# Moving the bursts of small matmuls, two transposes and the last output pieces in a fused attention and MLP kernel

## The chip, the core and the metric

The kernel runs on one core of a Trainium2 chip. The metric is device time in microseconds (us) from the program's start to its end. Before the change the median of three runs is 246.94 us (246.36 to 247.11). One further execution was taken with the hardware profiler; all durations below come from it.

The engines are named as in the profile: PE multiplies matrices (TensorE), with PEld loading its weights; DVE (VectorE) and ACT (ScalarE) read and write on-chip memory element by element; POOL (GpSimd) and SP (SyncE) here mostly issue DMA transfers. Each engine runs its instructions in program order and waits on semaphores of the others.

## The reference

There are 8 batches of 8 heads, 576 positions and head size 64, and 32 packed queries `p` per head. `sm_attn` is softmax attention with scale 1/8.

```python
p_packed = sm_attn(p, k, v)             # 32 x 64 per head
out = sm_attn(q, p_packed, p_packed)    # 576 x 64 per head
x = out.transpose(0, 2, 1, 3).reshape(4608, 512)
h = x @ w_in                            # 512 -> 2048
g = h * cos(h)
result = g @ w_out                      # 2048 -> 512, float32
```

All inputs are float32; the kernel casts them to bfloat16 while they are loaded.

## The kernel before, in words

**Per batch `b`.** A load brings k, q and v of the batch in (three DMAs issued by POOL, `load`, L92). k and q are needed transposed: batches 3 and up do it by a DMA transpose issued by SP (`xbar`, L96), k of batch 2 by PE (`pe_T`, L103) in three groups of eight 96x96 transposes, each group copied out of PSUM by DVE or ACT. `s1(b)` (L142) multiplies packed queries by k and ACT takes the exponential into `a1`. `a1` is transposed into `a1T`, from batch 3 on by a DMA transpose (`a1_xbar`, L158). `pp(b)` (L173) is the packed product, `a1T` by v: 48 small matmuls and two small copies into `pp_sb`; `pp_T` (L188) transposes it into `ppT`. `s2(b)` (L221) gives the second scores, `sums2` and `normalise` the normalised weights `a2n`. `ppw(b, n)` (L195) multiplies `ppT` by quarter n of `w_in`: 8 matmuls into one PSUM pair and one cast of 128x1024 into the columns 512n to 512n+511 of `PPW[b]`, so the second attention and `w_in` are folded into one matrix.

**A slot.** `slot(s, ...)` (L486) runs 16 steps, fc = 0 to 15, for batch s. Step fc computes the hidden block h(fc) on PE (`h_mm`, L250: four matmuls of 288 columns with columns 128·fc to 128·fc+127 of `PPW[s]`), its cosine on ACT (L261) and the product g(fc) on DVE (L264). So the `PPW` quarter n=2 is first needed at step 8. Between the hidden blocks PE does *out products*, the 128x512 matmuls of `g @ w_out` (L345) of the batch before, handed out one by one by `fill(n)`; 16 of them make one chunk of 128 output rows, which is copied out of PSUM into `osb` (by ACT inside a slot, by DVE between slots) and stored by two DMAs that SP issues. The slot spreads the out products over the steps by weights: `heavy={5: (5, 3)}` gives step 5 five extra shares, with 3 of its out products placed behind what hangs on that step.

**The burst.** `hooks` hang other work on a step. `tiled(s)` (L507) is the burst: `ppw(s, 2)` and `ppw(s, 3)`, 16 matmuls of a 64x32 form, then `pp(s+1)`, 48 of a 96x32 form, whose result goes into the spare columns of the hidden block's own PSUM pair (`spare`). In slot 2 it hangs on step 6, in slots 3 to 6 on step 5. ACT casts quarter 2, DVE does the two `pp_sb` copies and casts quarter 3.

**Between slots** come the `s2`, `sums2`, `normalise`, `ppw(b, 0)` and `ppw(b, 1)` of the next batch, the `s1` and `a1_xbar` of the one after, with out products between them. This stretch for batch 2 (L533 to L567) is written out by hand; L571 to L602 do it for the others.

**PSUM.** One pool of three pairs of banks (`psA`) is taken in rotation by everything but the out products: an allocation waits until the reader of the third one before it is done, so h(k) waits for g(k-3) if nothing came between. The out products have two banks of their own (`ot`).

**Queues.** SP issues stores and DMA transposes strictly in program order, and a wait of one holds all behind it. POOL issues the loads; before each set of three a one-element copy from `kT` of a later batch into `gate` (L528, L564, L588) holds POOL until that transpose has landed.

**The tail.** `tail_chunk` (L325) makes the last 128 rows in two pieces of 256 columns: 16 matmuls, a copy (ACT, then DVE) and two stores, one each from SP and ACT.

Of the kernel before, what the change touches and what calls it, by code (L numbers as in the profile page):

```python
# [8 lines left out]
FP32 = mybir.dt.float32  # L9
BF16 = mybir.dt.bfloat16  # L10
# [5 lines left out]
def kernel(  # L16
# [17 lines left out]
    TP = S // C  # L34
# [15 lines left out]
    O = ctx.enter_context(tc.tile_pool(name="psO", bufs=2, space=PSUM))  # L50
# [12 lines left out]
    V, ACT, G = nc.vector, nc.scalar, nc.gpsimd  # L63
# [5 lines left out]
    gate = const.tile([1, 1], BF16, name="gate")  # L69
# [10 lines left out]
    bf, xT, a1T, sums1, r1, rs1 = {}, {}, {}, {}, {}, {}  # L80
    a2u, lns, a2n, PPW = {}, {}, {}, {}

    def copy(eng, out, in_):
        if eng is ACT:
            ACT.copy(out=out, in_=in_)  # L85
        else:
            eng.tensor_copy(out=out, in_=in_)  # L87

    def psa(dt=FP32):
        return psum["A"].tile([128, 2, 512 if dt == FP32 else 1024], dt, name="psA", tag="A")  # L90

    def load(n, b):  # L92
        bf[n, b] = bf_pool.tile([TP, H, C * D], BF16, name=n + "bf", tag=n + "bf", bufs=1 if n == "q" else 2)
        G.dma_start(out=bf[n, b], in_=srcs[n][b].rearrange("h (p c) d -> p h (c d)", c=C))

    def xbar(n, b):  # L96
        t = xT[n, b] = att_pool.tile([128, H * 3, TP], BF16, name=n + "T", tag=n + "T", bufs=2 if n == "k" else 1)
        nc.sync.dma_start_transpose(out=t, in_=bf[n, b].rearrange("p h x -> p (h x)"))
# [4 lines left out]
    def pe_T(n, b, engs=(V, V, V), groups=(0, 1, 2), own=None):  # L103
        if 0 in groups:
            xT[n, b] = att_pool.tile([128, H * 3, TP], BF16, name=n + "T", tag=n + "T", bufs=2 if n == "k" else 1)
        t = xT[n, b]
        flat = bf[n, b].rearrange("p h x -> p (h x)")
        for i in groups:
            ps = own(BF16) if own else psa(BF16)[:, 0, :]
            for j in range(8):  # L110
                o = 8 * i + j
                nc.tensor.transpose(ps[:, j * TP:(j + 1) * TP], flat[:, o * 128:(o + 1) * 128],  # L112
                                    ident[0:TP, 0:TP])
            copy(engs[i], t[:, 8 * i:8 * i + 8].rearrange("p a x -> p (a x)"),
                 ps[:, 0:8 * TP])

    def bank(dt=FP32):
        return O.tile([128, 512 if dt == FP32 else 1024], dt, name="ot", tag="ot")
# [1 line left out]
    def pack_p(b0, b1, flat=None):  # L120
        ng = 2 * (b1 - b0)
        if flat is None:
            flat = psa(BF16).rearrange("p a x -> p (a x)")
        for g in range(ng):
            nc.tensor.transpose(flat[:, g * 128:(g + 1) * 128],
                                p_bf[:, 2 * b0 + g].rearrange("p t d -> p (t d)"), ident)
        V.tensor_copy(out=P2[:, b0:b1].rearrange("p b h n -> p (b h n)"), in_=flat[:, 0:ng * 128])
# [60 lines left out]
    def pp_T(b, eng=V, own=None):  # L188
        ps = own(BF16) if own else psa(BF16)[:, 0, :]
        t = pp_sb[b % 2].rearrange("p a d -> p (a d)")  # L190
        for i in range(2):
            nc.tensor.transpose(ps[:, i * 128:(i + 1) * 128], t[:, i * D:i * D + 128], ident)  # L192
        copy(eng, ppT[b % 2].rearrange("p i x n -> p (i x n)"), ps[:, 0:256])
# [98 lines left out]
    def h_rest(b):  # L292

        t = psa()
        for fc in range(NFC):
            for y in range(2):
                nc.tensor.matmul(t[:, fc // 8, (fc % 8) * 64:(fc % 8) * 64 + 64],
                                 PPW[b][:, y, fc * 128:(fc + 1) * 128], a2n[b][:, y, 512:576],
                                 start=(y == 0), stop=(y == 1))
        cs = cos_pool.tile([128, 2, 512], BF16, name="cosR", bufs=1)  # L300
        ACT.activation(out=cs, in_=t, func=AF.Sin, bias=PI_HALF)
        j0 = (b % 2) * 64
        V.tensor_tensor(out=joint[b // 2][:, :, j0:j0 + 64],
                        in0=t.rearrange("p a (f x) -> p (a f) x", x=64),
                        in1=cs.rearrange("p a (f x) -> p (a f) x", x=64), op=ALU.mult)
# [18 lines left out]

    def tail_chunk(b, c):  # L325
        osb = o_pool.tile([128, DM], FP32, name="osb")
        for i in range(2):
            cols = slice(i * 256, i * 256 + 256)
            ps = O.tile([128, 256], FP32, name="ot", tag="ot")
            for fc in range(NFC):  # L330
                nc.tensor.matmul(ps, joint[b // 2][:, fc, :], w_out_bf[:, fc, cols],  # L331
                                 start=(fc == 0), stop=(fc == NFC - 1))
            copy((ACT, V)[i], osb[:, cols], ps)
            for (a, z, rows), q in zip(pieces_of(b, c), (nc.sync, nc.scalar)):
                q.dma_start(out=rows[:, cols], in_=osb[a:z, cols])

# [25 lines left out]
    def fill(n):  # L362
        while n > 0 and filler:
            next(filler[0][0])
            filler[0][1] -= 1
            if filler[0][1] == 0:
                filler.pop(0)
            n -= 1
# [117 lines left out]
    def slot(s, hooks, keep=0, heavy={}, last=None):  # L486


        left = to_do() - keep
        weight = [1 + heavy.get(fc, (0, 0))[0] for fc in range(NFC)]  # L490
        for fc in range(NFC):
            rest = h_mm(s, fc)
            if fc == NFC - 1 and last:
                last()
            rest()
            quota = (left * sum(weight[:fc + 1])) // sum(weight) - (left + keep - to_do())
            behind = min(quota, heavy[fc][1]) if fc in heavy else quota
            fill(quota - behind)
            while hooks and hooks[0][0] == fc:
                hooks.pop(0)[1]()  # L500
            fill(behind)

    def pw2(b, n, eng=None):
        ppw(b, n, eng)
        ppw(b, n + 1, eng)

    def tiled(b):  # L507


        own, later = spare[0], []  # L510
        for n in (2, 3):
            later += ppw(b, n, (ACT, V)[n - 2], later=True)
        later[0]()
        pp(b + 1, V, own=lambda: own)
        later[1]()

    def tk(n, b, i):
        return lambda: pe_T(n, b, (ACT, V, ACT), (i,))

    def cross(n, b):  # L520
        return lambda: xbar(n, b)

    osb_eng[0] = ACT
    slot(1, [(2, lambda: pw2(1, 2, (ACT, V))), (4, lambda: h_rest(0)), (6, lambda: pack_p(2, 4)), (8, tk("k", 2, 0)), (9, tk("k", 2, 1)),
             (9, cross("q", 2)), (10, tk("k", 2, 2)), (12, cross("k", 3))], 4, {2: (1, 2), 4: (3, 5)})
    ACT.preload_act_table_set(EXP_SET)
    osb_eng[0] = V
    G.tensor_copy(out=gate, in_=xT["k", 3][0:1, 0, 0:1])  # L528
    load("v", 3)
    load("q", 3)  # L530
    load("k", 4)
# [6 lines left out]
    fill(3)  # L538
    a1_pe(2, (1,))
    recips(2)  # L540
    fill(5)
    pp(2)
    s1(3)
    a1_xbar(3)
    fill(3)
    pp_T(2)
    recips(3)
    fill(5)
    s2(2)
    ppw(2, 0, V)  # L550
    xbar("q", 3)
    xbar("k", 4)
    fill(3)
    sums2(2, 0)
    fill(3)
    sums2(2, 1)
    rest_ppw, = ppw(2, 1, (V, V), later=True)
    fill(2)
    normalise(2)
    ACT.preload_act_table_set(SIN_SET)  # L560
    rest_ppw()
    nc.sync.dma_start_transpose(out=P2[:, 4:B].rearrange("p b (t h) n -> p (b t) (h n)", t=2),
                                in_=p_bf[:, 8:2 * B].rearrange("p g t d -> p (g t d)"))
    G.tensor_copy(out=gate, in_=xT["k", 4][0:1, 0, 0:1])  # L564
    for n, b in (("v", 4), ("q", 4), ("k", 5)):
        load(n, b)
    fill(9)  # L567
    osb_eng[0] = ACT
    slot(2, [(6, lambda: tiled(2))], 10, {6: (5, 3)}, lambda: pp_T(3, V))

    for s in range(3, B):  # L571
        nxt = s + 1 < B
        ACT.preload_act_table_set(EXP_SET)
        osb_eng[0] = V
        set_filler(s - 1)
        fill(5)
        s2(s)
        ppw(s, 0, V)
        fill(8)
        if nxt:  # L580
            s1(s + 1)
            ppw(s, 1, V)
            a1_xbar(s + 1)
            xbar("q", s + 1)
            recips(s + 1)
            if s + 2 < B:
                xbar("k", s + 2)
                G.tensor_copy(out=gate, in_=xT["k", s + 2][0:1, 0, 0:1])  # L588
        else:
            for n in range(1, 4):  # L590
                ppw(s, n, V)
        fill(4 if nxt else 6)
        sums2(s, 0)
        fill(5)
        sums2(s, 1)
        normalise(s)
        ACT.preload_act_table_set(SIN_SET)
        fill(13)
        osb_eng[0] = ACT
        for n, b in (("v", s + 2), ("q", s + 2), ("k", s + 3)):  # L600
            if b < B:
                load(n, b)  # L602
        if nxt:
            slot(s, [(5, lambda: tiled(s))], 5 if s % 2 else 13, {5: (5, 3)}, lambda: pp_T(s + 1, V))
        else:
            slot(s, [], 5)
    set_filler(B - 1)
# [32 lines left out]
```

## Time and profile before

| what | us |
|---|---|
| median of three runs | 246.94 |
| the profiled execution, its whole time | 247.53 |
| its span, first to last instruction | 245.7 |
| PE busy | 232.0 |
| ACT busy | 166.6 |
| DVE busy | 162.4 |
| TensorE clock granted | 1.00 throughout |
| slot 2, its first hidden block | 74.95 |
| slot 3, its first hidden block | 101.71 |

Times in the text are counted from the start of the span. In a timeline a row gives start, length, engine, line, operation, tiles, shape and count; in brackets stands the idle time before it and what ended that. Matmuls are pipelined, and a matmul's length in a row includes its way through the array; what counts is the pitch from one start to the next: 216 ns for an out product, 122 ns for a matmul of 288 columns (0.49 us for a hidden block of four). Some matmul records are missing from a trace, so counts in rows may be one short of the program's. The chain of waits gives the work that ended last, in order of time, as start, length and name.

### The profile page before, as it was taken

Reading aid. Unit: us, or ns where it says so; the run is one execution under the profiler, and the core shown is the slowest. Engines: PE = TensorE matmul, PEld = TensorE weight load, DVE = VectorE, ACT = ScalarE, POOL = GpSimd, SP = SyncE. Lnnn points to the kernel's source line nnn. Section 1 sums busy time; section 2 is a strip of 40 time slices with the busy share of each in tenths; the row PEclk is TensorE's granted clock in tenths of the full one; section 3 lists DMA queues with packets and bytes.
Section 4 is the critical chain, followed back from the end, with each engine's and each line's share of the span. In section 5 each row is a group of like instructions: output and inputs, shape, how many; then the busy total and the mean of one; then the engine's idle time right before and its main releaser. Section 6 shows DMA issues by size and latency. Waiting matters only on the chain.

```text
span 245.7 us, 5424 instructions
## 1 busy us (share of the span) xinstructions
PE 232.0 (94%) x2204; PEld 128.4 (52%) x2239; DVE 162.4 (66%) x259; ACT 166.6 (68%) x267; POOL 38.1 (16%) x61
## 2 busy tenths in 40 slices
PE   7989889999999799999999999999999999999993
PEld 3463345566545464556455654656455645665452
DVE  3369987686459687578757875868656878784000
ACT  2359998767478587868786787858796766773110
POOL 8532330210130023004100510030100110011000
PEclk9999999999999999999999999999999999999999
DMA  6999999999789989999999799999292111311123
GB/s 87 204 210 207 204 208 227 200 240 149 167 121 185 215 182 197 215 204 174 163 191 237 134 214 207 189 161 179 56 194 51 37 45 43 85 39 49 54 74 85
DMA packets 63992, 37.37 MB, mean 152 GB/s; under 512 B 36592, under 2 KB 59376, under 8 KB 63968
## 3 DMA queue, kind: packets, MB, share of 16 engines
q0 software_dynamic: 23184, 18.81, 50.3%
q1 hardware_dynamic: 40624, 18.09, 35.9%
q8 instruction: 17, 0.28, 0.5%
q10 hardware_dynamic: 160, 0.13, 0.2%
q14 instruction: 7, 0.06, 0.1%
HBM read 37.22 MB, written 9.44 MB: 190 GB/s over the span
## 4 chain that ended last, share of the span: by engine, by line
PE 80%; DMA 13%; ACT 2%; issue 2%; DVE 1%; DVEq 0%
PE ot L345 45%; PE psA L257 21%; DMA qbf<-in_q_dram 7%; DMA a1T<-a 6%; PE ot L385 3%; PE psA L207 2%; PE psA L137 2%; PE psA L180 1%; PE ot L331 1%; PE psA L233 1%; PE psA L112 1%; ACT kT L85 1%; ACT a L146 1%; PE psA L192 0%; PE psA L170 0%
## 5 line engine op out<-in xcount | busy, mean ns | idle before, releaser
L345 PE MATMUL ot<-w_out_bf,gT 128*128 128x512 bf16 x483 | 127.3, 379 | 2.5 <-issue 2.1
L264 DVE TENSOR_TENSOR gT<-psA,cosT 128x576 bf16<-128x576 f32 x112 | 83.3, 757 | 19.5 <-ACT cosT L261 18.5
L261 ACT ACTIVATE cosT<-psA 128x576 bf16<-128x576 f32 x112 | 72.9, 652 | 24.8 <-PE psA L257 23.0
L257 PE MATMUL psA<-a2n,PPW 128*128 128x288 bf16 x448 | 73.3, 286 | 0.4 <-DVE gT L264 0.2
L345 PEld LDWEIGHTS <-gT 128*128 128x128 bf16 x512 | 48.1, 98 | 39.8 <-issue 4.4
L257 PEld LDWEIGHTS <-PPW 128*128 128x128 bf16 x448 | 43.7, 98 | 30.2 <-issue 0.6
L87 DVE CAST PPW<-psA 128x1024 bf16<-128x1024 f32 (+1 forms) x25 | 26.9, 1092 | 6.6 <-PE psA L207 6.4
L87 DVE COPY osb<-ot 128x512 f32<-128x512 f32 (+1 forms) x14 | 9.4, 670 | 20.6 <-PE ot L331 17.6
L85 ACT COPY osb<-ot 128x512 f32<-128x512 f32 (+1 forms) x23 | 13.2, 574 | 14.3 <-PE ot L345 13.2
L268 POOL COPY joint<-gT 128x512 bf16<-128x512 bf16 x14 | 8.6, 617 | 79.9 <-DVE gT L264 79.9
L243 DVE SCALAR_TENSOR_TENSOR a2n<-a2u,r,lns 128x576 bf16<-128x576 bf16 x16 | 12.4, 815 | 10.7 <-ACT lns L241 10.7
L146 ACT ACTIVATE a<-psA 128x576 bf16<-128x576 f32 x16 | 10.3, 646 | 7.8 <-PE psA L137 7.8
L235 ACT ACTIVATE lns<-psA 128x576 f32<-128x576 f32 x16 | 10.3, 650 | 7.2 <-PE psA L233 6.6
L345 PE MATMUL ot<-w_out_bf,joint 128*128 128x512 bf16 x47 | 12.0, 380 | 0.2
L225 ACT ACTIVATE a2u<-psA,rs 128x576 bf16<-128x576 f32 x16 | 11.0, 736 | 1.6 <-PE psA L137 1.4
L385 PE MATMUL ot<-wz 128*128 128x512 bf16 (+1 forms) x15 | 8.3, 660 | 2.0 <-DVE wz L399 1.7
L85 ACT CAST PPW<-psA 128x1024 bf16<-128x1024 f32 (+1 forms) x7 | 6.1, 891 | 5.8 <-PE psA L207 5.8
L241 ACT ACTIVATE lns<-lns 128x576 f32<-128x576 f32 x16 | 10.0, 674 | 0.0
L207 PE MATMUL psA<-w_in_bf,ppT 64*32 64x512 bf16 x224 | 9.8, 379 | 0.0
L289 DVE TENSOR_TENSOR gT<-psH,cosT 128x512 bf16<-128x512 f32 x15 | 9.3, 684 | 0.4 <-ACT cosT L288 0.4
L288 ACT ACTIVATE cosT<-psH 128x512 bf16<-128x512 f32 x15 | 8.4, 627 | 0.7 <-DVE gT L289 0.4
L588 POOL COPY gate<-kT 1x1 bf16<-1x1 bf16 x3 | 0.5, 181 | 50.8 <-DMA kT<-kbf 50.8
(92 smaller groups left out, 173.5 us busy)
## 6 DMA issues: line engine op xcount, KB each, us to landing
kbf<-in_k_dram POOLq DMA_DIRECT2D x8, 576.0 KB, 13.7
vbf<-in_v_dram POOLq DMA_DIRECT2D x8, 576.0 KB, 7.6
qbf<-in_q_dram POOLq DMA_DIRECT2D x8, 576.0 KB, 10.7
out_dram<-osb SPq DMA_DIRECT2D x24, 192.0 KB, 2.7
out_dram<-osb SPq DMA_DIRECT2D x22, 128.0 KB, 2.5
w_in_bf<-in_moe_w_in_dram POOLq DMA_DIRECT2D x4, 512.0 KB, 16.5
w_out_bf<-in_moe_w_out_dram POOLq DMA_DIRECT2D x4, 512.0 KB, 21.3
out_dram<-osb SPq DMA_DIRECT2D x26, 64.0 KB, 2.1
```

Of the source, the lines that this page charges most:

```text
L85: ACT.copy(out=out, in_=in_)
L87: eng.tensor_copy(out=out, in_=in_)
L146: ACT.activation(out=a1[b % 2][:, y, :, 0:TP].rearrange("p (e m) x -> p e m x", e=2), in_=ps[y][:, :, 0:HS].rearrange("p e (m x) -> p e m ...
L207: nc.tensor.matmul(ps[y][32 * x:32 * x + 32, :], ppT[b % 2][r, 0, x, :], w_in_bf[r, x, n * 512:(n + 1) * 512], start=True, stop=True)
L225: ACT.activation(out=a2u[b][:, y].rearrange("p (e x) -> p e x", e=2), in_=ps[y][:, :, 0:HS], func=AF.Exp, scale=rs1[b][:, y:y + 1])
L235: ACT.activation(out=lns[b][:, y].rearrange("p (e x) -> p e x", e=2), in_=ps[:, :, 0:HS], func=AF.Ln)
L243: V.scalar_tensor_tensor(out=a2n[b][:, y], in0=a2u[b][:, y], scalar=r1[b][:, y:y + 1], in1=lns[b][:, y], op0=ALU.mult, op1=ALU.mult)
L257: nc.tensor.matmul(ps[:, e, 0:HS], PPW[b][:, y, fc * 128:(fc + 1) * 128], a2n[b][:, y, e * HS:(e + 1) * HS], start=(y == 0), stop=(y == 1))
L261: ACT.activation(out=csv, in_=ps[:, :, 0:HS], func=AF.Sin, bias=PI_HALF)
L264: V.tensor_tensor(out=gT[b][:, fc, :].rearrange("p (e x) -> p e x", e=2), in0=ps[:, :, 0:HS], in1=csv, op=ALU.mult)
L345: nc.tensor.matmul(pss[c], w, w_out_bf[:, fc, :], start=(fc == 0), stop=(fc == NFC - 1))
L385: nc.tensor.matmul(wps, w[:, 0:128], w, start=True, stop=True)
```

## The change

- **Slots 3 to 6:** the burst `tiled(s)` hangs on step 7 in place of 5, with 4 out products behind it in place of 3.
- **Slot 2:** `ppw(2, 2)` and `ppw(2, 3)` stay on step 6, without `pp(3)`; quarter 2 is now cast by DVE and quarter 3 by ACT. `pp(3)` hangs alone on step 9, takes a PSUM pair of its own, and ACT does its two copies. The weights change to `{6: (3, 3), 9: (1, 1)}`.
- **k of batch 2 (slot 1):** groups 0 and 1 are both transposed at step 8, into the two halves of one PSUM pair, and then copied, one by ACT and one by DVE; group 2 stays on step 10. Step 9 has none any more.
- **Batch 2 between the slots:** seven out products in place of five before `pp(2)`, two for three and four for five behind it; `ppw(2, 1)` goes ahead of the second `sums2`, and DVE casts it whole at once, where it cast it in two halves after `normalise`. The total of out products is the same. On SP the two stores of one chunk now stand ahead of the transpose `a1T` of batch 3, where they stood behind it.
- **Batch 7:** one out product moves ahead of `ppw(7, 1)` to `ppw(7, 3)`.
- **Tail:** pieces of 256, 128 and 128 columns, copied by DVE, ACT, DVE; six stores for four.
- The `gate` copy gets a name, `behind`; its place and form are the same.

```diff
@@ pe_T
-            copy(engs[i], t[:, 8 * i:8 * i + 8].rearrange("p a x -> p (a x)"),
-                 ps[:, 0:8 * TP])
+            to = t[:, 8 * i:8 * i + 8].rearrange("p a x -> p (a x)"), ps[:, 0:8 * TP]
+            if engs[i] is None:
+                return to
+            copy(engs[i], *to)
@@ tail_chunk
-        for i in range(2):
-            cols = slice(i * 256, i * 256 + 256)
-            ps = O.tile([128, 256], FP32, name="ot", tag="ot")
+        for i, (a, z) in enumerate(((0, 256), (256, 384), (384, 512))):
+            cols = slice(a, z)
+            ps = O.tile([128, z - a], FP32, name="ot", tag="ot")
...
-            copy((ACT, V)[i], osb[:, cols], ps)
+            copy((V, ACT, V)[i], osb[:, cols], ps)
@@ slot 1
-    def tk(n, b, i):
-        return lambda: pe_T(n, b, (ACT, V, ACT), (i,))
+    def tk2():
+
+        t = psa(BF16)
+        later = []
+        for i in range(2):
+            later.append(pe_T("k", 2, (None,) * 3, (i,), own=lambda dt: t[:, i, :]))
+        for eng, (out, ps) in zip((ACT, V), later):
+            copy(eng, out, ps)
...
-    slot(1, [(2, lambda: pw2(1, 2, (ACT, V))), (4, lambda: h_rest(0)), (6, lambda: pack_p(2, 4)), (8, tk("k", 2, 0)), (9, tk("k", 2, 1)),
-             (9, cross("q", 2)), (10, tk("k", 2, 2)), (12, cross("k", 3))], 4, {2: (1, 2), 4: (3, 5)})
+    slot(1, [(2, lambda: pw2(1, 2, (ACT, V))), (4, lambda: h_rest(0)), (6, lambda: pack_p(2, 4)), (8, tk2),
+             (9, cross("q", 2)), (10, lambda: pe_T("k", 2, (V, V, ACT), (2,))), (12, cross("k", 3))], 4, {2: (1, 2), 4: (3, 5)})
@@ batch 2, between the slots
     recips(2)
-    fill(5)
+    fill(7)
     pp(2)
     s1(3)
     a1_xbar(3)
-    fill(3)
+    fill(2)
     pp_T(2)
     recips(3)
-    fill(5)
+    fill(4)
     s2(2)
...
     sums2(2, 0)
-    fill(3)
+    fill(1)
+    ppw(2, 1, V)
     sums2(2, 1)
-    rest_ppw, = ppw(2, 1, (V, V), later=True)
-    fill(2)
+    fill(4)
     normalise(2)
     ACT.preload_act_table_set(SIN_SET)
-    rest_ppw()
...
-    slot(2, [(6, lambda: tiled(2))], 10, {6: (5, 3)}, lambda: pp_T(3, V))
+    slot(2, [(6, lambda: pw2(2, 2)), (9, lambda: pp(3, ACT))], 10, {6: (3, 3), 9: (1, 1)}, lambda: pp_T(3, V))
@@ batches 3 to 7
-        fill(8)
+        fill(8 if nxt else 9)
...
-        fill(4 if nxt else 6)
+        fill(4 if nxt else 5)
...
-            slot(s, [(5, lambda: tiled(s))], 5 if s % 2 else 13, {5: (5, 3)}, lambda: pp_T(s + 1, V))
+            slot(s, [(7, lambda: tiled(s))], 5 if s % 2 else 13, {7: (5, 4)}, lambda: pp_T(s + 1, V))
```

More of the change, by code (lines that the diff above doesn't have):

```diff
@@ L94, in load, with behind @@
         G.dma_start(out=bf[n, b], in_=srcs[n][b].rearrange("h (p c) d -> p h (c d)", c=C))
+    def behind(t):
+        G.tensor_copy(out=gate, in_=t)
     def xbar(n, b):
@@ L523 @@
     osb_eng[0] = ACT
-    slot(1, [(2, lambda: pw2(1, 2, (ACT, V))), (4, lambda: h_rest(0)), (6, lambda: pack_p(2, 4)), (8, tk("k", 2, 0)), (9, tk("k", 2, 1)),
-             (9, cross("q", 2)), (10, tk("k", 2, 2)), (12, cross("k", 3))], 4, {2: (1, 2), 4: (3, 5)})
+    slot(1, [(2, lambda: pw2(1, 2, (ACT, V))), (4, lambda: h_rest(0)), (6, lambda: pack_p(2, 4)), (8, tk2),
+             (9, cross("q", 2)), (10, lambda: pe_T("k", 2, (V, V, ACT), (2,))), (12, cross("k", 3))], 4, {2: (1, 2), 4: (3, 5)})
     ACT.preload_act_table_set(EXP_SET)
     osb_eng[0] = V
-    G.tensor_copy(out=gate, in_=xT["k", 3][0:1, 0, 0:1])
+    behind(xT["k", 3][0:1, 0, 0:1])
     load("v", 3)
@@ L554 @@
     sums2(2, 0)
-    fill(3)
+    fill(1)
+    ppw(2, 1, V)
     sums2(2, 1)
-    rest_ppw, = ppw(2, 1, (V, V), later=True)
-    fill(2)
+    fill(4)
     normalise(2)
     ACT.preload_act_table_set(SIN_SET)
-    rest_ppw()
     nc.sync.dma_start_transpose(out=P2[:, 4:B].rearrange("p b (t h) n -> p (b t) (h n)", t=2),
                                 in_=p_bf[:, 8:2 * B].rearrange("p g t d -> p (g t d)"))
-    G.tensor_copy(out=gate, in_=xT["k", 4][0:1, 0, 0:1])
+    behind(xT["k", 4][0:1, 0, 0:1])
     for n, b in (("v", 4), ("q", 4), ("k", 5)):
@@ L587 @@
                 xbar("k", s + 2)
-                G.tensor_copy(out=gate, in_=xT["k", s + 2][0:1, 0, 0:1])
+                behind(xT["k", s + 2][0:1, 0, 0:1])
         else:
```

## The prediction

> **What bounds the kernel.** I read the page's busy times and its chain first, then PE's timeline stretch by stretch, then the rows of ACT, DVE and SP around each place that the change touches.
>
> ```profile
> PE 232.0 (94%) x2204; PEld 128.4 (52%) x2239; DVE 162.4 (66%) x259; ACT 166.6 (68%) x267; POOL 38.1 (16%) x61
> PE 80%; DMA 13%; ACT 2%; issue 2%; DVE 1%; DVEq 0%
> ```
>
> PE carries the chain. Between two hidden blocks PE's starts are as far apart as its pitches make them (216 ns an out product, 0.49 us a hidden block), so in such a stretch nothing can be won by moving work. Only the places count where a start comes late. Slot 1 has two, at the transposes of k:
>
> ```profile
> 53.40 0.65 PE L257 MATMUL psA<-a2n,PPW 128*128 128x288 bf16 x4
> 54.21 0.50 PE L112 MATMUL psA<-ident,kbf 96*128 96x96 bf16 x8 [0.16 <-ACT kT L85]
> ...
> 54.98 0.65 PE L257 MATMUL psA<-a2n,PPW 128*128 128x288 bf16 x4
> 55.58 0.50 PE L112 MATMUL psA<-ident,kbf 96*128 96x96 bf16 x8
> ```
>
> Four matmuls from 53.40 end by pitch at 53.89, and the transposes start at 54.21: 0.32 late. From 54.98 to 55.47, start at 55.58: 0.11 late. Slot 2 has two more:
>
> ```profile
> 76.89 0.59 PE L345 MATMUL ot<-w_out_bf,gT 128*128 128x512 bf16 x2
> 77.65 0.65 PE L257 MATMUL psA<-a2n,PPW 128*128 128x288 bf16 x4 [0.16 <-DVE gT L264]
> ...
> 81.86 0.63 PE L207 MATMUL psA<-w_in_bf,ppT 64*32 64x512 bf16 x16
> 83.68 0.56 PE L180 MATMUL psA<-vbf,a1T 96*32 96x64 bf16 x48 [1.20 <-DMA a1T<-a]
> ```
>
> Two out products end at 77.32, h(3) starts at 77.65: 0.33 late, because g(0) is late on DVE. And `pp(3)` starts 1.82 us after its burst began. In slot 3 the same two rows, without a wait, are 0.55 apart, so 1.27 us is the wait for `a1T`:
>
> ```profile
> 106.38 1.46 PE L345 MATMUL ot<-w_out_bf,gT 128*128 128x512 bf16 x6
> 107.77 0.63 PE L207 MATMUL psA<-w_in_bf,ppT 64*32 64x512 bf16 x16
> 108.32 0.55 PE L180 MATMUL psA<-vbf,a1T 96*32 96x64 bf16 x48
> ...
> 109.47 0.65 PE L257 MATMUL psA<-a2n,PPW 128*128 128x288 bf16 x4
> ```
>
> Slots 3 to 6 show no late start by pitch. The chain has the transfer that `pp(3)` waits for, issued at 69.22 and landed at 83.63:
>
> ```profile
> 69.22 14.41 DMA a1T<-a
> ```
>
> **k of batch 2: minus 0.43.** With groups 0 and 1 in one pair at step 8, what held group 1, the pair of h(8) still read by g(8), is gone; its 16 transposes need the pair of `pack_p`, copied by 52.2. h(9) then starts at 53.74 (52.62, 0.69 of transposes, two out products) and needs g(7), over by 53.13; h(10) starts at 54.66 and needs g(8), over by 54.26; group 2 at 55.15 needs the copies of groups 0 and 1, ACT's over by 54.2 and DVE's (0.55, behind g(8)) by 54.8. All are there, so 0.32 + 0.11 goes. Bounds: 0 to 0.43 gained.
>
> **Batch 2 between the slots: 0.** `pp(2)` and `s1(3)` come 0.43 earlier by slot 1 and two out products (0.43) later: the same clock time, 67.46 for `s1(3)`. That matters, since k of batch 3 lands only at 67.33 (SP issued its transpose at 61.13, set by loads). So `a1T` of batch 3 is ready to issue at 69.22 as before. Ahead of it on SP now stand two stores. Their chunk ends with the last product but one before `pp(2)`, DVE copies it from 66.8 to 67.5 (ahead of `pp_sb`, which is ready at 67.58), and two issues take 1.0 (before, they held SP for 1.08 at 74.25, behind `a1T`): SP is free at 68.7. From `s2(2)` on all is 0.43 early. `ppw(2, 1)` needs the pair that ACT's second exponential frees 0.02 before PE gets there: 0 to 0.1 lost, 0 taken.
>
> **Slot 2.** Start of h(0): 74.95 - 0.43 = 74.52.
> - DVE no longer casts two halves of 0.68 between `normalise` and g(0); their whole cast (1.22) lies in DVE's idle 1.88 before `normalise`. g(0) starts when its cosine is done, and the 0.33 goes.
> - `pp(3)` alone. The merged burst takes PE from 107.68 (106.38 and six pitches) to 108.82 (109.47 less three out products): 1.14. `ppw` pairs alone, in slot 1:
>
> ```profile
> 42.57 0.81 PE L345 MATMUL ot<-w_out_bf,gT 128*128 128x512 bf16 x3
> 43.31 0.63 PE L207 MATMUL psA<-w_in_bf,ppT 64*32 64x512 bf16 x16
> 44.09 0.38 PE L345 MATMUL ot<-w_out_bf,gT 128*128 128x512 bf16 x1 [0.16 <-issue]
> ```
>
> 43.22 to 43.87 (one out product's record is missing before 44.09): 0.65. `pp` alone: 0.09 to get in (as at 43.22), 0.36 from first to last start, 0.14 out as in the merged burst: 0.59. Together 1.24, so +0.10; with the exit of the `ppw` pair (0.31) in place of 0.14 it is +0.27; less than 0 cannot be, as nothing is left out. The Trainium skill speaks against this split: "TensorEngine Tiling (Array Packing)", Key Properties, says that a change of tiling mode drains the array. The 0.09 and 0.31 at the edges agree that a change costs, and the row prices it. The page "TensorE: Matmul & The Clock Gate", Single matmul latency, puts a drain at about 175 ns; two more changes would be 0.35 by it, an estimate, and the sum 0.25 poorer.
> - The wait for `a1T`. The steps in slot 2 are now 0.49 + 1.5 x 0.216. Up to step 6: h(6) at 4.88 after h(0) (six blocks, nine out products), burst at 6.11, h(7) at 7.32, h(8) could start at 8.03.
> - A new wait: quarter 2, needed by h(8), is now cast by DVE behind g(6). The rows for it, from slot 3:
>
> ```profile
> 108.25 1.01 ACT L85 CAST PPW<-psA 128x1024 bf16<-128x1024 f32 x1 [0.91 <-PE psA L207]
> 108.95 0.42 DVE L87 CAST pp_sb<-psA 128x128 bf16<-128x128 f32 x2 [0.82 <-PE psA L180]
> 109.29 1.22 DVE L87 CAST PPW<-psA 128x1024 bf16<-128x1024 f32 x1
> 110.16 0.65 ACT L261 ACTIVATE cosT<-psA 128x576 bf16<-128x576 f32 x1 [0.90 <-PE psA L257]
> 110.84 0.76 DVE L264 TENSOR_TENSOR gT<-psA,cosT 128x576 bf16<-128x576 f32 x1 [0.33 <-ACT cosT L261]
> ```
>
> A cosine starts 0.69 after its hidden block, g 0.68 after the cosine. A chunk copy falls between the cosines of steps 5 and 6 and delays the latter to 5.77; g(6) from 6.45, DVE free at 7.17, cast done at 8.39, 0.08 for the signal: h(8) at 8.47, 0.44 late. Without the chunk copy in the way it is 0.24, with another 0.25 of queueing 0.7; I take 0.44. What is queued behind h(8) on PE is the rest of the slot; the product `pp(3)` comes two blocks and four out products later, at 10.4, clock time 84.9. That is 1.3 after `a1T` landed. The two stores ahead of it put 256 KB in front on the same queue, 1.3 us at the page's 200 GB/s: even that just fits. So the 1.27 goes; bounds 0.7 to 1.27.
> - ACT's copies of `pp_sb` (0.32 + 0.29, rows of batch 1) in place of DVE's 0.42: their first reader is six blocks off, cover enough; the pair they hold is needed by h(12). h(15) gave `pp_T` a 0.13 wait (DVE behind); with DVE lighter I take half, 0.07.
>
> Slot 2 in all: -0.33 - 1.27 + 0.10 + 0.44 - 0.07 = -1.13.
>
> **Slots 3 to 6: 0.** The burst is the same 1.14, later. Covers that shrink: quarter 2 was cast three steps before h(8), now in the step before. ACT starts it 0.48 after the burst begins (107.77 to 108.25) and is done at 1.49; h(8) starts at 1.70 + 0.22 (the fourth out product) = 1.92: 0.35 spare after the signal. In slots 4 and 6 a chunk ends with the product just before the burst, its copy delays the cast by 0.14: 0.2 spare. `pp_sb` is free at 1.60, also in time. Nothing to gain, as no start is late now; 0 to 0.2 each to lose. `a1T` of batch 4 landed at 107.46 (issue 97.66, 9.80 to landing), 0.86 ahead of its use; PE comes 1.56 early, two blocks and three out products (1.63) late, so that use stays at 108.4.
>
> **Batch 7: 0**, PE has no late start at 201.4 and DVE's casts end before the pairs are wanted (205.1 for h(0) at 207.9).
>
> **Tail: minus 0.1.** Matmul time is the same (0.109 a piece of 256; transposes of 128 columns with a weight load each run at 0.056, so +0.05). DVE's last copy is 128x128 (0.29 by `pp_sb`'s row) for 128x256 (0.43): -0.14; the stores' landing, 1.95 to 2.22, I take as unchanged (64 KB against 128 KB loads nothing here). Bounds -0.25 to +0.15. The skill's "DMA: Bandwidth & Descriptors", opening table, wants 512 B at least for line rate; rows of 128 floats are just that, no run here shows it.
>
> **Sum:** -0.43 - 1.13 - 0.1 = -1.66. Profiled execution: 247.53 - 1.66 = 245.87. It lies 0.59 above the median, so the median becomes 246.94 - 1.66 = **245.3**.
>
> **Rivals.**
> - *`a1T` is late again at step 9.* Loads of three tensors share the engines with it, and the stores now go first. For: the landing was 14.41 against 9.80 in batch 4. Against: 1.3 of room. Landing 2 us later puts back 0.7: 246.0. Chance 0.15.
> - *The gain is handed back in slot 3.* Loads and transposes keep their clock times while PE is 1.56 early, and every set of loads is gated by a transpose. If `a1T` of batch 4 lands 1 to 1.6 us later than now, the burst waits 0.1 to 0.7, and with a full-size h(8) wait the total is about -0.7: 246.3. For: the room was only 0.86. Against: the later step restores it. Chance 0.13.
> - *Slower: h(8) waits in all four slots 3 to 6.* One step is left between cast and use. It must lose 0.41 in each slot to eat the gain and 0.6 to show as slower, that is, ACT's cast must end 0.95 later than slot 3's row gives it, about a chunk copy and half a cosine in the queue. At 0.65: -1.66 + 2.6, 247.9. For: ACT also has those copies. Against: it idles 0.91 before the cast. Chance 0.09.
> - The forecast holds 0.63.
>
> **How the numbers follow.** 0.3% is 0.74 us, about what three runs spread here, and what can be told from no change. All lesser terms at their good ends give -2.4 (244.5), and the forecast with h(8), slot 1 and the tail at their bad ends -0.7 (246.2). The range takes in the first two rivals and some of the third's low end: 244.4 to 246.9; alone the forecast has 244.5 to 246.2. Faster: 0.62 of the forecast, 0.12 of the first rival, 0.04 of the second: 0.78. Slower: 0.09. The rest, 0.13, is the same.
>
> **What would show it.** In the changed profile: no idle of PE on `a1T`, group 1 of k at its pitch, h(3) of slot 2 at its pitch, and a wait of some 0.4 before h(8) of slot 2 on DVE's cast; slots 3 to 6 without a wait on ACT's cast. I am wrong if PE idles at step 8 of those slots, or at `pp(3)` or `pp(4)` on a DMA.

## The result, and the profile after

The changed kernel takes 245.56 us (median of 12 runs, 245.24 to 247.04) against 247.04 us for the kernel before in the same comparison (median of 12 runs, 246.28 to 248.01). The ratio is 0.995 with a 95% interval of 0.9928 to 0.9971, that is 0.7 to 1.8 us faster. In a second comparison, made beside the last experiments, the same program had 245.59 us (7 runs) and a ratio of 0.9934 (0.9908 to 0.9961). The forecast was 245.3.

The profiled execution took 246.25 us for 247.53 before, its span 244.5 for 245.7. The line numbers are now some four to twelve higher: an out product is L351, a hidden block L263, `ppw` L213, `pp` L186, a transpose of k L116. From the page of the changed kernel:

```profile
PE 231.6 (95%) x2220; PEld 128.6 (53%) x2255; DVE 162.2 (66%) x257; ACT 166.8 (68%) x269; POOL 38.1 (16%) x61
PE 76%; DVE 6%; DMA 5%; issue 2%; ACT 1%; ACTq 0%
```

PE has the same work in a shorter span. The DMA share that is left in the chain is `a1T` of batch 4 (12.51 us), of which more below. Then PE's timeline of the changed kernel, first in slot 1:

```profile
53.18 0.84 PE L116 MATMUL psA<-ident,kbf 96*128 96x96 bf16 x16
53.86 0.60 PE L351 MATMUL ot<-w_out_bf,gT 128*128 128x512 bf16 x2
54.30 0.65 PE L263 MATMUL psA<-a2n,PPW 128*128 128x288 bf16 x4
...
55.22 0.65 PE L263 MATMUL psA<-a2n,PPW 128*128 128x288 bf16 x4
55.71 0.51 PE L116 MATMUL psA<-ident,kbf 96*128 96x96 bf16 x8
```

All 16 transposes run in one go, and group 2 starts at the pitch (55.22 + 0.49). Both late starts of slot 1 are gone. Slot 2 of the changed kernel, in the same view:

```profile
76.72 0.65 PE L263 MATMUL psA<-a2n,PPW 128*128 128x288 bf16 x4
77.21 0.38 PE L351 MATMUL ot<-w_out_bf,gT 128*128 128x512 bf16 x1
77.42 0.65 PE L263 MATMUL psA<-a2n,PPW 128*128 128x288 bf16 x4
...
81.20 0.62 PE L213 MATMUL psA<-w_in_bf,ppT 64*32 64x512 bf16 x16
81.76 0.82 PE L351 MATMUL ot<-w_out_bf,gT 128*128 128x512 bf16 x3
82.42 0.65 PE L263 MATMUL psA<-a2n,PPW 128*128 128x288 bf16 x4
82.91 0.38 PE L351 MATMUL ot<-w_out_bf,gT 128*128 128x512 bf16 x1
83.40 0.66 PE L263 MATMUL psA<-a2n,PPW 128*128 128x288 bf16 x4
...
85.35 0.56 PE L186 MATMUL psA<-vbf,a1T 96*32 96x64 bf16 x48
```

h(3), at 77.42, starts at its pitch; `pp(3)`, at 85.35, waits for nothing (its `a1T` landed at 84.14). In their place stands one new late start: the out product at 82.91 is over by 83.13, and h(8) starts at 83.40, 0.28 late. DVE's rows give the reason:

```profile
81.45 0.76 DVE L270 TENSOR_TENSOR gT<-psA,cosT 128x576 bf16<-128x576 f32 x1 [0.27 <-ACT cosT L267]
82.13 1.21 DVE L87 CAST PPW<-psA 128x1024 bf16<-128x1024 f32 x1
```

The cast of quarter 2 stands behind g(6) and ends at 83.34. And slot 3 has a wait that the kernel before did not have. `pp(4)` starts 0.81 after its burst began, for 0.55 without a wait:

```profile
108.30 0.63 PE L213 MATMUL psA<-w_in_bf,ppT 64*32 64x512 bf16 x16
109.11 0.55 PE L186 MATMUL psA<-vbf,a1T 96*32 96x64 bf16 x48 [0.19 <-DMA a1T<-a]
```

### A clock for all the runs

The executions differ in their first 50 us, where the program is the same: the first matmul of `pack_p` in slot 1, a place in front of every edit, starts between 50.08 and 51.95 us in the 13 profiles of this study. In some the chain of waits goes through the load of q of an early batch there (before and e7: 50.27 and 50.08), in others through work of DVE (changed and e11: 50.83 and 51.11); in e4, the latest, the granted clock was 0.91 from 10 to 20 us and 0.94 from 20 to 35 us, where the others had 1.00. Why they part stays open. Counted from that matmul, PE's later stages agree to 0.01 us where nothing waits for a transfer. So the table gives the time from it to the first matmul of `s2(2)`, `s2(3)` and `s2(4)`, to the first of the tail and, where it was recorded, to the last landing. All are read off PE's timeline and the landings of the stores.

| kernel | starts at | `s2(2)` | `s2(3)` | `s2(4)` | tail | last landing |
|---|---|---|---|---|---|---|
| before | 50.27 | 19.48 | 43.19 | 69.12 | 187.82 | 194.24 |
| changed | 50.83 | 19.05 | 41.53 | 67.72 | 186.42 | 192.54 |
| changed, again (e10) | 50.22 | 19.11 | 41.60 | 67.53 | 186.22 | 192.35 |
| e1, slot 2 put back | 50.85 | 19.05 | 42.84 | 68.76 | 187.46 | 193.59 |
| e2, bursts at step 5 | 50.33 | 19.05 | 41.54 | 68.44 | 187.13 | not recorded |
| e3, k in three groups | 50.26 | 19.48 | 41.97 | 67.90 | 186.59 | 192.72 |
| e4, tail put back | 51.95 | 19.05 | 41.53 | 67.46 | 186.17 | 192.59 |
| e5, late cast | 50.20 | 19.05 | 41.88 | 67.81 | 186.52 | 192.66 |
| e6, casts swapped | 50.95 | 19.05 | 41.25 | 67.18 | 185.88 | 192.01 |
| e11, the same again | 51.11 | 19.05 | 41.25 | 67.18 | 185.88 | 192.02 |
| e7, slot 3 split too | 50.08 | 19.05 | 41.25 | 67.22 | 185.92 | 192.05 |
| e8, five, three, five | 50.29 | 19.05 | 41.53 | 67.46 | 186.15 | 192.29 |
| e9, last piece of 64 | 50.91 | 19.05 | 41.53 | 67.46 | 186.16 | 192.43 |

From before to changed: up to `s2(2)` 0.43 less; from there to `s2(3)` 22.48 for 23.71, 1.23 less; to `s2(4)` 26.19 for 25.93, 0.26 more; from `s2(4)` to the tail 118.70 both; tail to last landing 6.12 for 6.42, 0.30 less. In all 1.70 less. The last landings differ by only 1.14 (244.51 and 243.37) and the whole times of the two profiled executions by 1.28, since the changed one reached slot 1 0.56 later, in code that is the same.

### The profile page after: what moved, and what is told of

It reads as the page before. It is cut to its first block, busy times and chain, and to the rows that moved or that the text cites. A ratio compares the mean times of both kernels' runs of the same rounds, so it can differ in the third digit from the quotient of the medians.

```text
span 244.5 us, 5460 instructions
## 1 busy us (share of the span) xinstructions
PE 231.6 (95%) x2220; PEld 128.6 (53%) x2255; DVE 162.2 (66%) x257; ACT 166.8 (68%) x269; POOL 38.1 (16%) x61
## 4 chain that ended last, share of the span: by engine, by line
PE 76%; DVE 6%; DMA 5%; issue 2%; ACT 1%; ACTq 0%
PE ot L351 45%; PE psA L263 21%; DMA a1T<-a 5%; DVE gT L295 3%; PE psA L213 3%; PE psA L143 2%; PE ot L337 1%; PE psA L239 1%; DVE PPW L87 1%; PE psA L186 1%; ACT cosT L294 0%; PE psA L116 0%; DVE qT L87 0%; PE psA L303 0%; DVE a1T L87 0%
## 5 line engine op out<-in xcount | busy, mean ns | idle before, releaser
L351 PE MATMUL ot<-w_out_bf,gT 128*128 128x512 bf16 x485 | 128.9, 379 | 1.8 <-issue 1.3
L263 PE MATMUL psA<-a2n,PPW 128*128 128x288 bf16 x448 | 73.4, 286 | 0.6 <-issue 0.2
L351 PEld LDWEIGHTS <-gT 128*128 128x128 bf16 x512 | 48.2, 98 | 39.7 <-issue 4.6
L263 PEld LDWEIGHTS <-PPW 128*128 128x128 bf16 x448 | 43.7, 98 | 30.5 <-DVE PPW L87 0.5
L87 DVE COPY osb<-ot 128x512 f32<-128x512 f32 (+2 forms) x15 | 9.7, 645 | 20.4 <-PE ot L337 17.2
L351 PE MATMUL ot<-w_out_bf,joint 128*128 128x512 bf16 x45 | 11.5, 379 | 0.3 <-issue 0.2
L213 PE MATMUL psA<-w_in_bf,ppT 64*32 64x512 bf16 x224 | 9.8, 379 | 0.1
L289 PE MATMUL psH<-a2n,PPW 128*128 128x512 bf16 x28 | 7.3, 381 | 1.0 <-DVE PPW L87 0.8
```

What stands on the lines that cost most here:

```text
L213: nc.tensor.matmul(ps[y][32 * x:32 * x + 32, :], ppT[b % 2][r, 0, x, :], w_in_bf[r, x, n * 512:(n + 1) * 512], start=True, stop=True)
L263: nc.tensor.matmul(ps[:, e, 0:HS], PPW[b][:, y, fc * 128:(fc + 1) * 128], a2n[b][:, y, e * HS:(e + 1) * HS], start=(y == 0), stop=(y == 1))
L351: nc.tensor.matmul(pss[c], w, w_out_bf[:, fc, :], start=(fc == 0), stop=(fc == NFC - 1))
```

## The experiments

Each is the changed kernel with one edit. The measured times are medians beside the kernel before, with the ratio to it; the verdicts rest on the table.

### Slot 2 put back into one burst (e1)

```diff
-slot(2, [(6, lambda: pw2(2, 2)), (9, lambda: pp(3, ACT))], 10, {6: (3, 3), 9: (1, 1)}, lambda: pp_T(3, V))
+slot(2, [(6, lambda: tiled(2))], 10, {6: (5, 3)}, lambda: pp_T(3, V))
```

> The changed kernel with slot 2 put back: one burst of ppw(2,2), ppw(2,3) and pp(3) at step 6. Theory (the split takes pp(3) past the landing of a1T): in the changed kernel the burst of step 6 begins at 81.2 and a1T of batch 3 lands at 84.1, so pp(3), 0.55 after the burst's start, waits about 2.3 us; the split's own price (0.10) and the wait of h(8) on DVE's cast (0.28) go. Net 1.9 us slower than the changed kernel. Rival (the wait was worth only what it cost before the change): the wait is 1.3 us, net 0.9 slower. Second rival (the transfer moves with PE): no wait, 0.4 faster.

Measured: 246.57 us, ratio 0.9977 (0.9955 to 1.0), and 1.31 more from `s2(2)` to `s2(3)`. PE's timeline of this kernel:

```profile
81.66 0.63 PE L213 MATMUL psA<-w_in_bf,ppT 64*32 64x512 bf16 x16
83.91 0.56 PE L186 MATMUL psA<-vbf,a1T 96*32 96x64 bf16 x48 [1.62 <-DMA a1T<-a]
```

`pp(3)` starts 2.25 after the burst, 1.70 of it a wait (0.55 without). So the wait comes back, and the split is what takes it away; the second rival falls. Its size lies between the first expectation's 2.3 and the rival's 1.3, and so does the net, 1.31 for 1.9 and 0.9. The expectation put the burst at 81.2; the merged burst has six out products in front of it for three, and one fewer before h(6), and began at 81.66, and `a1T` landed at 83.86 for the 84.1 taken. How far the 1.70 exceeds the 1.27 of before is a matter of the execution, too: over the profiles this landing lies between 82.69 and 84.62 (83.63 before). But every landing recorded is behind 82.21, where this burst wanted `a1T`. The bill closes: 1.70, less the 0.28 of h(8), which is gone here, less the 1.31, leaves 0.11 for the split itself. PE's rows of the changed kernel say the same: counted by pitch, the `ppw` pairs take PE 0.65 (81.11 to 81.76) and `pp(3)` 0.59 (85.25 to 85.85 with the out product behind it left out), 1.24 for the 1.14 of the merged burst.

### The bursts of slots 3 to 6 at step 5 again (e2)

```diff
-slot(s, [(7, lambda: tiled(s))], 5 if s % 2 else 13, {7: (5, 4)}, lambda: pp_T(s + 1, V))
+slot(s, [(5, lambda: tiled(s))], 5 if s % 2 else 13, {5: (5, 3)}, lambda: pp_T(s + 1, V))
```

> The changed kernel with the bursts of slots 3 to 6 back at step 5, three out products behind. Theory A (the later step is what keeps most of slot 2's gain): a1T of batch 4 landed at 109.07 in the changed kernel and pp(4) waited 0.26 for it at step 7; at step 5 pp(4) would be wanted 1.63 earlier, so it waits some 1.9 us, 1.6 us slower than the changed kernel; slots 4 to 6 unchanged. Theory B (the prediction's zero for this part, taken by itself): within 0.3 us of the changed kernel, since no burst of slots 3 to 6 waited before the change.

Measured: 246.7 us, ratio 0.9986 (0.9957 to 1.0015); 26.90 from `s2(3)` to `s2(4)` where 25.93 is the time without a wait. PE's timeline of this kernel:

```profile
106.17 0.62 PE L213 MATMUL psA<-w_in_bf,ppT 64*32 64x512 bf16 x16
107.70 0.55 PE L186 MATMUL psA<-vbf,a1T 96*32 96x64 bf16 x48 [0.91 <-DMA a1T<-a]
```

`pp(4)` waits 0.98 (1.53 less 0.55). Theory A holds in kind; the size was read from an execution in which `a1T` of batch 4 landed at 109.07, here it landed at 107.66. Theory B falls: where nothing waits the step costs and wins nothing (slot 3 takes 25.93 at step 5 before the change and at step 7 in e3), but with slot 2 faster the later step is what keeps the gain. Slots 4 to 6 take the same time in both.

### k of batch 2 in three groups (e3)

```diff
-(8, tk2), (9, cross("q", 2)), (10, lambda: pe_T("k", 2, (V, V, ACT), (2,)))
+(8, lambda: pe_T("k", 2, (ACT, V, ACT), (0,))), (9, lambda: pe_T("k", 2, (ACT, V, ACT), (1,))),
+(9, cross("q", 2)), (10, lambda: pe_T("k", 2, (ACT, V, ACT), (2,)))
```

> The changed kernel with the three groups of k of batch 2 back at steps 8, 9 and 10, each in a pair of its own. Theory: the waits of 0.32 and 0.11 us at groups 1 and 2 return and nothing hides them, so PE reaches slot 2 0.43 later; as pp(4) then comes 0.43 later too, its wait of 0.26 for a1T of batch 4 goes. Net 0.17 us slower than the changed kernel, 0.43 if that transfer moves along. Rival (s1(3) is set by the landing of k of batch 3 and not by PE): no difference up to s1(3), net 0.

Measured: 246.03 us, ratio 0.9954 (0.9935 to 0.9974), which the total cannot tell from the changed kernel. PE's timeline of this kernel has the late start back (53.39 + 0.49 = 53.88, then 54.20):

```profile
53.39 0.65 PE L263 MATMUL psA<-a2n,PPW 128*128 128x288 bf16 x4
54.20 0.50 PE L116 MATMUL psA<-ident,kbf 96*128 96x96 bf16 x8 [0.16 <-ACT kT L85]
```

The 0.43 stands in `s2(2)` (19.48) and is still there at `s2(3)` (41.97 for 41.53); the rival falls. `pp(4)` did not wait, so in the end it is 0.17 against the first execution of the changed kernel, as expected.

### The tail of two pieces (e4)

```diff
-enumerate(((0, 256), (256, 384), (384, 512)))   ...   copy((V, ACT, V)[i], osb[:, cols], ps)
+enumerate(((0, 256), (256, 512)))               ...   copy((ACT, V)[i], osb[:, cols], ps)
```

> The changed kernel with the tail of before, two pieces of 256 columns copied by ACT and DVE. From the two traces (last landing 6.43 us after the first matmul of the tail before, 6.13 after): 0.30 us more. From the prediction: 0.1 us more.

Measured: 246.38 us, ratio 0.9965 (0.9942 to 0.9988). Tail to last landing 6.42 for 6.12: the 0.30. ACT's last stores and DVE's last copy, before the change and in the changed kernel:

```profile
240.48 2.32 ACTq L335 DMA_DIRECT2D out_dram<-osb  x2
241.83 0.43 DVE L87 COPY osb<-ot 128x256 f32<-128x256 f32 x1 [17.65 <-PE ot L331]
...
240.67 1.39 ACTq L341 DMA_DIRECT2D out_dram<-osb  x2
240.98 0.29 DVE L87 COPY osb<-ot 128x128 f32<-128x128 f32 x1 [1.31 <-PE ot L337]
```

The copy starts 3.75 and 3.74 after the tail's first matmul (238.08 and 237.24) and is 0.14 shorter; the last store is issued on ACT 0.03 behind it in both and lands 2.22 and 2.07 after that.

### The second `ppw` of batch 2 late again (e5)

```diff
-fill(1)
-ppw(2, 1, V)
-sums2(2, 1)
-fill(4)
+fill(3)
+sums2(2, 1)
+rest_ppw, = ppw(2, 1, (V, V), later=True)
+fill(2)
 normalise(2)
 ACT.preload_act_table_set(SIN_SET)
+rest_ppw()
```

> The changed kernel with ppw(2,1) back behind the second sums2 of batch 2 and its cast back as two halves behind normalise (three, two and nine out products around it as before). Counted from the first matmul of pack_p in slot 1, s2(3) began at 41.53 us in the changed kernel. Theory: the two halves (2 x 0.68 on DVE) put g(0) of slot 2 back, h(3) starts 0.33 late as before the change, and nothing gives it back: s2(3) at 41.9. Rival (the order did not matter, the 0.33 came from the chunk copy on DVE): s2(3) at 41.5.

Measured: 246.3 us, ratio 0.9962 (0.994 to 0.9984); `s2(3)` at 41.88, 0.35 later. The theory holds. DVE's rows, and PE's, in this kernel (the cast in two halves, the chunk copy behind it, then g(0); and h(3)):

```profile
74.55 1.28 DVE L87 CAST PPW<-psA 128x512 bf16<-128x512 f32 x2
75.75 0.68 DVE L87 COPY osb<-ot 128x512 f32<-128x512 f32 x1
76.34 2.93 DVE L270 TENSOR_TENSOR gT<-psA,cosT 128x576 bf16<-128x576 f32 x4
...
77.15 0.65 PE L263 MATMUL psA<-a2n,PPW 128*128 128x288 bf16 x4 [0.20 <-DVE gT L270]
```

### The casts of slot 2 swapped (e6 and e11)

```diff
+def pw2r(b, n):
+    ppw(b, n, ACT)
+    ppw(b, n + 1, V)
-slot(2, [(6, lambda: pw2(2, 2)), ...
+slot(2, [(6, lambda: pw2r(2, 2)), ...
```

> The changed kernel with the casts of slot 2 swapped: quarter 2 by ACT, quarter 3 by DVE. Theory: h(8) of slot 2, 0.28 late in the changed kernel for DVE's cast behind g(6), finds its quarter cast, since ACT is free 0.3 before; nothing else is late in its place: s2(3) at 41.25 after the first matmul of pack_p (41.53 in the changed kernel). Rival (ACT's next cosine or DVE's g(7), behind its own cast of 1.22, makes h(9) or h(10) late): 41.4 to 41.6.

> The changed kernel with the casts of slot 2 swapped, once more beside the changed kernel. Theory: 0.28 us faster than the changed kernel (s2(2) to s2(3) 22.20 for 22.48), and 0.28 less room for a1T of batch 4. Rival: the lost room is paid in the wait at pp(4), no difference in the whole.

Measured: 245.78 us, ratio 0.9928 (0.9899 to 0.9958), and again, beside the changed kernel, 245.44 against 245.59, ratios 0.9938 (0.991 to 0.9966) and 0.9934 (0.9908 to 0.9961). `s2(2)` to `s2(3)` is 22.20 in both, 0.28 less, and PE's timeline (e6) has h(8) at its pitch:

```profile
82.55 0.65 PE L263 MATMUL psA<-a2n,PPW 128*128 128x288 bf16 x4
83.04 0.38 PE L351 MATMUL ot<-w_out_bf,gT 128*128 128x512 bf16 x1
83.25 0.65 PE L263 MATMUL psA<-a2n,PPW 128*128 128x288 bf16 x4
```

In neither execution did `pp(4)` wait (25.93). A difference of 0.28 in the total lies within the intervals; on the table's clock it is there to 0.01.

### Five, three and five out products around `pp(2)` (e8)

```diff
-fill(7)   pp(2) s1(3) a1_xbar(3)   fill(2)   pp_T(2) recips(3)   fill(4)
+fill(5)   pp(2) s1(3) a1_xbar(3)   fill(3)   pp_T(2) recips(3)   fill(5)
```

> The changed kernel with five, three and five out products around pp(2) and pp_T(2), as before, in place of seven, two and four; the two stores of that chunk stand behind a1T of batch 3 on SP again. Theory (k of batch 3, landed at 67.1 to 67.3, is the bound of s1(3)): s1(3) would come at 16.74 after the first matmul of pack_p, 0.43 earlier than the changed kernel's 17.17, and waits for k where PE is early; s2(2) 0 to 0.3 later than the changed kernel's 19.05. Rival (the stores ahead of a1T cost time): a1T of batch 3 lands some 1 us earlier, no effect on PE since pp(3) has 1.2 to spare. Rival 2 (the order has no effect at all): s2(2) at 19.05.

Measured: 245.83 us, ratio 0.9946 (0.9918 to 0.9974). Counted from `pack_p`, `s1(3)` came 0.43 earlier; it started at 67.02, after k of batch 3 (66.83), and did not wait; `s2(2)` at 19.05. The order had no effect on PE here: the second rival. `a1T` of batch 3 landed at 83.01, in the two executions of the changed kernel at 84.14 and 83.99. That the stores ahead of it made the difference is not shown: in all 13 profiles SP issues this transpose 1.79 after `s1(3)` starts, with the stores ahead of it or behind, and in e4, e7 and e9, which have them ahead, it landed at 82.69 to 82.94.

That k can be the bound is shown by the second execution of the changed kernel (e10), whose table row has `s2(2)` 0.06 late. There `s1(3)` starts at 67.45, 0.55 behind `pp(2)`, where e8 and the first execution have 0.48, and POOL's `gate` copy, which waits for the same landing, starts with it:

```profile
67.45 0.44 PE L143 MATMUL psA<-kT,P 64*32 64x288 bf16 x16
...
67.46 0.18 POOL L98 COPY gate<-kT 1x1 bf16<-1x1 bf16 x1 [4.65 <-DMA kT<-kbf]
```

With five, three and five, `s1(3)` would have been wanted there 0.5 before k. So this edit is worth nothing in the execution that was profiled; that it is worth something in one like e10's is likely, but was not run.

### A last piece of 64 columns (e9)

```diff
-enumerate(((0, 256), (256, 384), (384, 512)))
+enumerate(((0, 256), (256, 448), (448, 512)))
```

> The changed kernel with tail pieces of 256, 192 and 64 columns. The last landing was 6.42 us after the tail's first matmul with two pieces of 256 and 6.12 with a last piece of 128. Theory (the last copy and the last store's bytes set the end): DVE's copy of 128x64 takes 0.22 in place of 0.29, the landing some 0.07 less: 5.98. Rival (rows of 256 bytes cost the store more than rows of 512): 6.12 or more.

Measured: 246.14 us, ratio 0.9941 (0.9911 to 0.9971); tail to last landing 6.27 for 6.12, later, not earlier. Of this kernel's timeline, the last stores of SP and ACT and DVE's last copy:

```profile
239.53 2.31 SPq L341 DMA_DIRECT2D out_dram<-osb  x3
...
240.73 1.38 ACTq L341 DMA_DIRECT2D out_dram<-osb  x2
240.81 0.23 DVE L87 COPY osb<-ot 128x64 f32<-128x64 f32 x1 [1.31 <-PE ot L337]
```

The copy is over at 241.04, as the theory has it. But the two queues were still issuing the stores of the piece before (issued at 240.73, 0.5 us each), and the last ones went out only at 241.29 and 241.33. The rival's reason is not what is seen: the store of 256-byte rows landed 2.01 after its issue on ACT, that of 512-byte rows 2.07. The Trainium skill's "DMA: Bandwidth & Descriptors", Specifications, asks for 512 bytes at least for line rate; in a store of 16 KB at the end of the program these runs show no loss below that.

### Once more, and slot 3 split as slot 2 (e10 and e7)

```diff
-slot(s, [(7, lambda: tiled(s))], 5 if s % 2 else 13, {7: (5, 4)}, lambda: pp_T(s + 1, V))
+slot(s, [(7, lambda: tiled(s))] if s > 3 else [(6, lambda: pw2r(s, 2)), (9, lambda: pp(s + 1, ACT))],
+     5 if s % 2 else 13, {7: (5, 4)} if s > 3 else {6: (3, 3), 9: (1, 1)}, lambda: pp_T(s + 1, V))
```

(e7, with the swap of e6; e10 has no edit.)

> The changed kernel once more, beside the next two. In its first profile pp(4) waited 0.26 for a1T of batch 4 (s2(3) to s2(4) 26.19); in three other kernels with the same slots 2 and 3 it did not (25.93). Theory (the transfer's landing differs by 1 to 2 us between executions and has about 0 to 0.9 us of room): s2(3) to s2(4) between 25.93 and 26.3 in this one. Rival (the wait belongs to this program): 26.19 again.

> The changed kernel with the casts of slot 2 swapped, and slot 3 made like slot 2: ppw(3,2) and ppw(3,3) at step 6, pp(4) alone at step 9, its two copies by ACT. Theory: pp(4) moves some 1.6 us later and cannot wait any more; the split costs 0.10 as in slot 2: s2(3) to s2(4) 26.03 in every execution. So it is 0.10 slower than the swap alone where a1T is in time, and faster where it is late by more than 0.10. Rival (the pair that pp(4) takes makes h(10) or h(11) wait): 26.1 to 26.4.

Measured: e10 245.59 us, 25.93 from `s2(3)` to `s2(4)`: no wait at `pp(4)`. It starts 0.55 after its burst in PE's timeline:

```profile
107.76 0.63 PE L213 MATMUL psA<-w_in_bf,ppT 64*32 64x512 bf16 x16
108.31 0.56 PE L186 MATMUL psA<-vbf,a1T 96*32 96x64 bf16 x48
```

The 0.26 belongs to an execution, not to the program.

e7 took 245.23 us, ratio 0.992 (0.9889 to 0.9951), the lowest median of the study; its interval overlaps those of the two beside it. PE's timeline of e7:

```profile
106.13 0.63 PE L213 MATMUL psA<-w_in_bf,ppT 64*32 64x512 bf16 x16
...
109.99 0.56 PE L186 MATMUL psA<-vbf,a1T 96*32 96x64 bf16 x48
```

In this execution `a1T` of batch 4 landed at 109.14. At step 7 `pp(4)` would have been wanted at 107.83 (57.75 after the first matmul of `pack_p`, as in e11) and would have waited 1.3, if the landing had been the same; here it had 0.85 to spare. Without a wait the split costs slot 3 0.04 (25.97 for 25.93) and not 0.10, since the 0.07 that h(15) and `pp_T` lose to DVE at the end of slot 3 is no longer there.

## Why the prediction was right, point by point

- **k of batch 2: -0.43.** Measured -0.43, and shown by its undoing (e3).
- **Batch 2 between the slots: 0.** Measured 0.00, or +0.06 where k of batch 3 was late (e10), a wait that the prediction had seen near (67.46 for 67.33) and priced at nothing. Its 0 to 0.1 stood for another, of `ppw(2, 1)` for its pair: from `s2(2)` to h(0) it is 5.21 for 5.20. The two stores ahead of `a1T` held up nothing that the runs show: its issue follows `s1(3)` by 1.79 in every profile. `pp(3)` started 1.2 after the landing, for the 1.3 worked out.
- **DVE's early cast: -0.33.** Measured 0.35 by its undoing (e5).
- **The wait for `a1T`: -1.27.** Gone whole. Put back into the changed kernel it was 1.70 in the execution profiled (e1), so there the split is worth 1.31.
- **The split itself: +0.10.** Measured 0.11. The Trainium skill's "TensorEngine Tiling (Array Packing)", Key Properties, has a change of tiling mode drain the array. The runs show that a change costs, not why; the row of the trace gave its size, and the 0.25 more worked out with the page's drain is not there.
- **The new wait of h(8): +0.44.** The mechanism is the one told, on the cast told; measured 0.28 (shown by e6). The chunk copy delayed the cosine of step 6 by less (0.78 after h(6), for the 0.89 of the step), and the cast followed g(6) by 0.68 for 0.72.
- **The end of slot 2: -0.07.** Wrong. h(15) and `pp_T` still lose 0.13; lighter DVE did not help.
- **Slots 3 to 6: 0.** From `s2(4)` to the tail, batch 7 with its moved out product included, the two kernels take the same 118.70, and slot 3 without the wait for `a1T` the same 25.93. So h(8) never waits for ACT's cast: the rival that would have made it slower has no trace of itself. At `pp(4)` the second rival came about in small: 0.26 in one execution, 0 in the other. That idle of PE at `pp(4)` on a DMA is one of the signs by which the prediction said it would be wrong; here it holds for one execution of two. The prediction took the landing as 107.5 in clock time and the use as 108.4. The landings were 107.37 to 109.14 over all profiles, so the room is there or not, by the execution; with the burst at step 5 it is not (e2).
- **Tail: -0.1.** Measured -0.30, the term that was mis-sized most. The copy gave the 0.14 told. The 0.05 for more matmuls of 128 columns is not there (the last copy starts 3.74 after the first matmul, for 3.75). The step took the landing as unchanged; the last store landed 2.07 after its issue for 2.22, 0.15 less. (The sizes written there, 64 and 128 KB, are wrong: they are 32 and 64 KB.)

The sum was -1.66. Without a wait at `pp(4)` the terms measure -0.43 - 1.23 - 0.30 = -1.96, with the 0.26 -1.70. That it comes so near the sum is partly luck: the tail (0.20 more gained than told) and h(8) (0.16 less late) made up for the 0.26 at `pp(4)` and the 0.07 at the end of slot 2. The total time shows 0.7 to 1.8 less, as it also carries the differences of the first 50 us.

## What to carry to other kernels

When PE runs at its pitch, list the places where a start comes late by the pitch and price only those; the size of a wait on a transfer is no property of its place, since the landing does not follow PE (PE came to `pack_p` at 51.95 in e4 and at 50.22 in e10, and `a1T` of batch 4 landed at 107.59 and 107.57), so each gain in front of it makes the wait longer. An edit that is worth nothing by itself (the burst two steps later) can be what keeps the gain of another. Where executions differ in their first part, count from a matmul in front of the edits: as long as no transfer is waited for, a difference of 0.1 us can then be read off one profile of each, which the total does not show in ten runs.

## What the runs showed of the hardware that was not expected

- A transfer of one program lands at times that differ by 1.5 us between executions: `a1T` of batch 4 at 109.07 and 107.57 in two executions of the changed kernel, 107.37 to 109.14 over all profiles, while PE's stages between waits agree to 0.01 us.
- A store is not sooner done for being small if its queue is still issuing the one before: with 64 columns the copy ended at 241.04 and the stores went out at 241.29 and 241.33, each queue having taken about 0.5 us for the one in front.
- The last store landed 0.15 us sooner at 32 KB than at 64 KB (2.07 and 2.22 after its issue on ACT).
